# Four heads' 64-key remainders as one unit, and scales for two pairs of heads at once, in a fused attention and MoE kernel

## The chip, the cores and the metric

The kernel runs on one core of a Trainium2 chip. The metric is the device time of one execution in microseconds; the profile shows one such execution, engine by engine. The engines are TensorE (PE for its matmuls, PEld for its weight loads), VectorE (DVE), ScalarE (ACT), GpSimd (POOL) and SyncE (SP), whose queue issues nearly all DMAs. Each engine works through its own queue in order; between engines, semaphores hold an instruction back until what it reads has been written and the buffer that it writes is free.

## What is computed

Attention with a sigmoid in the place of the softmax, for 8 batches, 12 heads, 448 positions and 64 elements per head, and behind it a layer of two matrix products with an odd function between them:

```
scores = matmul(q, k.T) / sqrt(64) - log(448)
attn   = 1 / (1 + exp(-scores))
x      = matmul(attn, v)            # heads side by side: 3584 x 768
h      = x @ w_in                   # 768 x 2048
out    = (h - tanh(h)) @ w_out      # 2048 x 768
```

All arrays are float32.

## The kernel before

**Precision.** A product is made of float16 parts: each operand is scaled by a power of two and split into a high and a low half, and three products (high with high, high with low, low with high) are summed. The scale comes from the operand's sum of squares. In batch 0, and for the products with the attention weights of batch 1, float32 matmuls are used.

**Stages.** Batch 0's attention (`attention32`) and its first layer (`moe1_32`) run while the weights arrive and are converted. From then on the stages alternate: the first layer of a batch (`moe1`, 54.6 us) and its second layer (`moe2`). The attention of the *next* batch runs inside the second layer: a generator, `stream`, yields after each block of attention, and `second` calls it at fixed steps of the second layer. A step is six matmuls on the output tile `po`; a stage has 48 of them, three groups of 16, and then a remainder, `por`. The table `BLOCKS = (8, 12, 16, ..., 52)` sets the steps of the twelve blocks of a batch; tables of their own serve the second layers of batches 0 and 1. So the order of the work is written by hand, on TensorE, ScalarE, VectorE and GpSimd alike; only SyncE's queue is ordered by the build.

**A pair of heads.** Two heads of 64 elements fill the 128 partitions, and attention goes by pairs, numbered g. The 448 keys of a pair are cut into three chunks of 128 keys (c = 0, 1, 2) and a remainder of 64 (c = 3). For a chunk, `scores` issues for each of the three products one matmul per head: 64 rows of the array each, all 128 columns, into a PSUM tile `sc` of two banks. For the remainder each head has one corner of the array, 64 rows by 64 columns, so that the two heads use two corners of four, and fill one bank of `sc`. `weigh` (L386) takes the sigmoid on ScalarE, `split_a` makes the halves `ahl` (L393 on ScalarE, L394 on VectorE), and `av` multiplies them with V into the PSUM tile `acc`; there too the remainder uses two corners of four. `evac_x` moves `acc` to memory and squares it.

**Two blocks a pair.** In the first block of pair g stand the chunks 0 and 1, the product with V of all four parts of pair g-1, its `evac_x`, the float16 parts of Q of pair g+1 (`parts`, L346 and L349) and those of V. In the second stand `scales` of pair g+2, the chunk 2 and the remainder of pair g, the parts of K of pair g+2, and the sums of squares of pair g+3 (`norms`, L316: ScalarE, three instructions).

**Parts and scales.** `parts` writes both halves into a tile `w`, of which there is one buffer for K and Q alike (`tag="w", bufs=1`), and a DMA (L351) transposes it into `K` or `Q`. The high half of Q is always written by ScalarE (L346), that of K by VectorE (L348) from batch 2 on; the low half by VectorE (L349). `scales` (L324 to L337) adds a pair's sums over the partitions with a small matmul into the PSUM tile `pbn`, which ScalarE reads (L326), and makes the scales with five small operations on VectorE. The sums that it uses were taken a whole pair earlier.

**Between the groups of 16 steps**, ScalarE (L823) and VectorE (L824) empty the two `po` tiles; `po` has two buffers in all, and the next group needs both.

Of the kernel before, what the change touches and what calls it, by code (L numbers as in the profile page):

```python
# [19 lines left out]
P = 128  # L20
# [14 lines left out]
class Builder:  # L35
# [254 lines left out]
    def load_v(self, b, j, pool, tag, bufs):  # L290
        t = pool.tile([P, 2 * QT + 1, D], F32, name="vn", tag=tag, bufs=bufs)
        for h in range(2):
            src = self.v[b, 2 * j + h]
            self.nc.sync.dma_start(
                t[:, h * QT : (h + 1) * QT], src[: QT * P].rearrange("(c p) d -> p c d", c=QT)
            )
            self.nc.sync.dma_start(t[h * D : (h + 1) * D, 2 * QT], src[QT * P :])
        return t
# [8 lines left out]
    def norms(self, loaded):  # L307

        n = len(loaded)
        ss = self.sums.pop(0)  # L310
        self.sums.append(ss)
        for i, t in enumerate(loaded):
            flat = t.rearrange("p a b d -> p (a b d)" if i < 2 else "p a d -> p (a d)")
            rows, size = flat.shape
            junk = self.sm.tile([P, 8 * D], BF16, name="sqn", tag="sq", bufs=4)
            self.nc.scalar.activation(junk[:rows, :size], flat, AF.Square, accum_out=ss[:rows, i : i + 1])  # L316
        return ss[:, :n]

    def scales(self, ss):

        nc = self.nc
        n = ss.shape[1]
        pb = self.ps.tile([P, 512], F32, name="pbn", tag="tr", bufs=1)[:, :n]
        nc.tensor.matmul(pb, self.onesf, ss, start=True, stop=True)  # L324
        t = self.sm.tile([P, 3], F32, name="tn")
        nc.scalar.activation(t[:, :n], pb, AF.Relu, bias=self.tiny, scale=2.1)  # L326
        y = self.pow2(t[:, :n], n, "n")
# [4 lines left out]
        r = self.sm.tile([P, 2], F32, name="rn", bufs=5)  # L332
# [23 lines left out]
    def prep_v(self, vn, s):  # L356
        nc = self.nc
        flat = vn.rearrange("p c d -> p (c d)")
        v = self.att.tile([P, 2, 2 * QT + 1, D], F16, name="vhl", tag="vhl", bufs=3)
# [5 lines left out]
    def scores(self, c, K, Q):  # L365

        nc = self.nc
        ps = self.ps.tile([P, 2, 512], F32, name="sc", tag="sc", bufs=2)
        prods = ((0, 0), (0, 1), (1, 0)) if K.dtype == F16 else ((0, 0),)
        for n, (w, x) in enumerate(prods):  # L370
            for h in range(2):
                r = slice(h * D, (h + 1) * D)
                o = ps[:, h, : self.S] if c < QT else ps[r, 0, : self.S]
                nc.tensor.matmul(  # L374
                    o,
# [66 lines left out]
    def stream(self):  # L442
# [10 lines left out]
        def load(g):  # L453
            if g < G:
                qk[g] = self.load_qk(*at(g))
                if splits(g):
                    v[g] = self.load_v(*at(g), self.nat, "vn", 2)
# [528 lines left out]
```

## Time and profile before

| | |
|---|---|
| median of 3 runs | 1251.36 us (1249.97 to 1251.57) |
| the profiled execution | 1252.35 us, of which the span from the first to the last instruction is 1250.0 us |
| mean granted clock of TensorE | 0.993 of full speed |
| PE busy | 97% of the span |
| DVE, ACT busy | 74%, 73% |
| first layer of a batch | 54.6 us |
| second layer with the attention of the next batch | 87.8 us |

The page gives the busy time of each engine, and the chain of work that ended last, followed back from the last instruction. A row of a group names the line, the engine, the operation, what it writes and reads, and how often; then the busy time, the mean of one, and the idle time just before them with what ended it. A row of the timeline gives start and length in us and, in brackets, the idle time of the engine before it and what ended that. A matmul's length in such a row is that of its way through the array; the next one starts long before it ends, so rates are read from starts.

### The profile page before, as it was taken

How to read it: one execution, taken by the hardware profiler on the slowest of the kernel's cores; microseconds unless marked ns; L12 is line 12 of the kernel's file. 1: busy time of each engine (PE TensorE's matmuls, PEld its weight loads, DVE VectorE, ACT ScalarE, POOL GpSimd, SP SyncE). 2: the span in 40 equal slices, each digit the busy share in tenths (PEclk: the TensorE clock that was granted, in tenths of full speed). 3: DMA queues.
4: the chain of work that ended last, by engine and by line, in shares of the span. 5: the costliest groups of instructions: out<-in, count | busy, mean ns of one | idle time of the engine just before them, and what ended most of it. 6: DMA issues, size and time to landing. Idle time of an engine off the chain costs nothing.

```text
span 1250.0 us, 20037 instructions
## 1 busy us (share of the span) xinstructions
PE 1209.4 (97%) x7675; PEld 627.3 (50%) x7675; DVE 920.4 (74%) x1476; ACT 910.7 (73%) x1325; POOL 37.8 (3%) x38
## 2 busy tenths in 40 slices
PE   9899878999999999999999999999999999999998
PEld 3234433455545555555555555555555555555555
DVE  4889987878965698667976689557975779636930
ACT  5767786968888688886887688786888767854820
POOL 0100000000000000100001000000000000000000
PEclk9999989999999999999999999999999999999999
DMA  8973358220044300542034400552024400300000
GB/s 206 281 205 90 82 123 217 59 64 1 12 109 99 85 1 16 109 100 44 1 71 102 93 2 4 100 109 57 1 58 99 90 22 1 72 21 20 1 14 32
DMA packets 226448, 89.79 MB, mean 72 GB/s; under 512 B 214704, under 2 KB 216496, under 8 KB 226352
## 3 DMA queue, kind: packets, MB, share of 16 engines
q1 hardware_dynamic: 225424, 88.29, 30.2%
q8 instruction: 60, 0.98, 0.3%
q10 hardware_dynamic: 928, 0.23, 0.1%
q14 instruction: 36, 0.29, 0.1%
HBM read 58.20 MB, written 11.01 MB: 55 GB/s over the span
## 4 chain that ended last, share of the span: by engine, by line
PE 79%; ACT 7%; DVE 7%; DMA 3%; issue 2%; SPq 1%; DVEq 0%; ACTq 0%
PE ph L679 31%; PE po L794 26%; PE sc L374 7%; PE acc L405 7%; PE por L832 5%; PE ph L709 2%; ACT a L386 2%; DMA raw<-moe_w_in 1%; ACT wo L215 1%; DMA qn<-q 1%; DVE g L664 1%; DVE m L753 1%; DVE m L767 1%; DVE wo L218 1%; DVE m L764 1%
## 5 line engine op out<-in xcount | busy, mean ns | idle before, releaser
L794 PE MATMUL po<-wo,g 128*128 128x384 f16 x2304 | 394.1, 327 | 4.8 <-DVE o L824 2.6
L679 PE MATMUL ph<-xhl,wi 128*128 128x448 f16 x2016 | 382.6, 352 | 0.0
L794 PEld LDWEIGHTS <-g 128*128 128x128 f16 x2304 | 220.2, 98 | 180.9 <-issue 41.5
L679 PEld LDWEIGHTS <-wi 128*128 128x128 f16 x2016 | 196.7, 98 | 185.0 <-issue 1.8
L394 DVE SCALAR_TENSOR_TENSOR ahl<-a,ahl 128x896 f16<-128x896 f32 (+1 forms) x144 | 138.8, 1004 | 71.2 <-ACT ahl L393 71.2
L386 ACT ACTIVATE a<-sc,nls,rn 128x896 f32<-128x896 f32 (+1 forms) x168 | 163.5, 997 | 36.3 <-PE sc L374 34.4
L749 ACT ACTIVATE u<-ph,ih 128x896 f32<-128x896 f32 x64 | 64.3, 1005 | 94.6 <-PE ph L679 91.0
L374 PE MATMUL sc<-Q,K 64*128 64x448 f16 x1008 | 116.7, 356 | 8.8 <-ACT a L386 6.9
L393 ACT ACTIVATE ahl<-a 128x896 f16<-128x896 f32 (+1 forms) x144 | 114.7, 846 | 0.4 <-DVE n_y L98 0.4
L753 DVE SCALAR_TENSOR_TENSOR m<-ph,ihk,u 128x896 f32<-128x896 f32 x64 | 73.6, 1151 | 42.7 <-ACT th L751 42.4
L349 DVE SCALAR_TENSOR_TENSOR w<-qn,sn,w 112x512 f16<-112x512 f32 x42 | 31.5, 750 | 87.0 <-ACT w L346 87.0
L405 PE MATMUL acc<-ahl,vhl 128*64 128x448 f16 (+1 forms) x864 | 93.0, 356 | 0.4 <-DVE ahl L394 0.4
L663 ACT ACTIVATE g<-m,Sg 128x896 f16<-128x896 f32 x64 | 66.6, 1041 | 34.0 <-DVE m L767 28.7
L767 DVE COPY_PREDICATED m<-u,th 128x896 f32<-128x896 uint32 x64 | 77.4, 1209 | 6.9 <-DVE m L764 0.5
L664 DVE SCALAR_TENSOR_TENSOR g<-m,Sg,g 128x896 f16<-128x896 f32 x64 | 73.6, 1149 | 8.4 <-ACT g L663 8.3
L764 DVE SCALAR_TENSOR_TENSOR m<-q,m 128x896 f32<-128x896 f32 x64 | 69.9, 1093 | 9.9 <-ACT q L763 2.2
L709 PE MATMUL ph<-x,wi 128*128 128x448 f32 x192 | 75.1, 540 | 0.3 <-DVE x L417 0.3
L374 PEld LDWEIGHTS <-K 64*128 64x128 f16 x1008 | 41.3, 97 | 66.5 <-issue 39.3
L754 DVE SCALAR_TENSOR_TENSOR th<-ph,ih,th 128x896 f32<-128x896 f32 x64 | 73.4, 1147 | 0.0
L766 ACT ACTIVATE u<-u,b 128x896 f32<-128x896 f32 x64 | 66.7, 1043 | 5.9 <-DVE m L753 4.0
L760 DVE SCALAR_TENSOR_TENSOR m<-q,m 128x896 f32<-128x896 f32 x64 | 69.7, 1089 | 0.0
L405 PEld LDWEIGHTS <-vhl 128*64 128x64 f16 (+1 forms) x864 | 42.7, 108 | 48.7 <-issue 26.7
(131 smaller groups left out, 1228.3 us busy)
## 6 DMA issues: line engine op xcount, KB each, us to landing
raw<-moe_w_in SPq DMA_DIRECT2D x24, 512.0 KB, 5.9
rawo<-moe_w_out SPq DMA_DIRECT2D x32, 384.0 KB, 4.1
kn<-k SPq DMA_DIRECT2D x96, 112.0 KB, 2.8
qn<-q SPq DMA_DIRECT2D x94, 112.0 KB, 2.9
vn<-v SPq DMA_DIRECT2D x96, 96.0 KB, 2.5
out<-o SPq DMA_DIRECT2D x21, 384.0 KB, 2.4
vn<-v SPq DMA_DIRECT2D x96, 16.0 KB, 2.2
out<-orem SPq DMA_DIRECT2D x16, 96.0 KB, 2.2
```

The source lines that it names most:

```text
L374: nc.tensor.matmul(o, K[r, w, c * P : min((c + 1) * P, self.S)], Q[r, x, :], start=(n == 0), stop=(n == len(prods) - 1),)
L386: self.nc.scalar.activation(a, ps[:, :n, : self.S], AF.Sigmoid, bias=self.nls, scale=scale)
L393: nc.scalar.activation(A[:, 0], a, AF.Copy, scale=A_SCALE)
L394: nc.vector.scalar_tensor_tensor(A[:, 1], a, A_SCALE, A[:, 0], op0=ALU.mult, op1=ALU.subtract)
L405: self.nc.tensor.matmul(acc[o, : self.S], v[k, w, j], A[k, x, i], start=(c == 0 and n == 0), stop=(c == QT and n == len(prods) - 1),)
L664: nc.vector.scalar_tensor_tensor(g[:, 1], m, Sg, g[:, 0], op0=ALU.mult, op1=ALU.subtract)
L679: nc.tensor.matmul(ph[:, e, :S], self.wi[:, c * self.NB + k, part, e * P : (e + 1) * P], xhl[c][:, x, :], start=(i == 0), stop=(i == 3 * s ...
L709: nc.tensor.matmul(ph[:, e, :S], self.where("in", c)[:, f * P : (f + 1) * P], xs[c], start=(c == 0), stop=(c == self.NC - 1),)
L753: V.scalar_tensor_tensor(m, ps, ihk, u, op0=ALU.mult, op1=ALU.mult)
L764: V.scalar_tensor_tensor(m, q2, C2, m, op0=ALU.add, op1=ALU.mult)
L767: V.copy_predicated(m, u.bitcast(U32), th)
L794: nc.tensor.matmul(po[i][:, :H], gs[f // 2][:, x, f % 2, tk * P : (tk + 1) * P], self.wo[:, i * self.NF + f, w], start=(f == 0 and n == 0) ...
```

## The change

Attention goes by two pairs of heads, g (even) and h = g+1.

- The remainders of the two pairs are one unit: the four heads' 64 keys take the four corners of the array, head by rows and pair by columns, and fill both banks of one `sc` tile. Sigmoid and halves work on a full tile. In the product with V the four corners add into two `acc` tiles, of g and h, open at the same time: that of an even pair in the PSUM buffer `av`, that of an odd pair in `tr`.
- The remainder of h is computed with g's, in g's second block; so K and Q of h have to be there by then.
- One call of `scales` serves two pairs; the larger of the two sums sets the scale. Its `pbn` lies in the buffer `av` (for batch 1 in `sc`).
- V's remainder rows of both pairs are loaded with the even pair's tile.
- The blocks are still two a pair, at the same steps. Per two pairs there are now four, called B1 to B4 here:

```
B1  chunks 0, 1 of g;  product with V of h-2 (three chunks);  evac of h-2;  parts of V of h;  sums of V of g+2
B2  chunk 2 of g and the four-corner unit;                                   sums of K, Q, V of g+3
B3  scales of g+2 and g+3;  chunks 0, 1 of h;  product with V of g and of the unit;  evac of g;  parts of K, then Q, of g+2
B4  chunk 2 of h;  parts of K, then Q, of g+3;  parts of V of g+2;  sums of K, Q of g+4
```

The core of the diff:

```diff
@@ scores
-        for n, (w, x) in enumerate(prods):
-            for h in range(2):
-                r = slice(h * D, (h + 1) * D)
-                o = ps[:, h, : self.S] if c < QT else ps[r, 0, : self.S]
...
+        m = P // len(K)
+        for n, (w, x) in enumerate(prods):
+            for i in range(len(K)):
+                for h in range(2):
+                    r = slice(h * D, (h + 1) * D)
+                    self.nc.tensor.matmul(
+                        ps[i * m : (i + 1) * m, h, : self.S],
+                        K[i][r, w, c * P : c * P + m],
+                        Q[i][r, x, :],
...
@@ scales
+        nc.vector.tensor_tensor(u[:, :n], t[:, :n, 0], t[:, :n, 1], op=ALU.max)
...
@@ stream: the blocks
+        for g in range(0, G, 2):
+            h = g + 1
+            early = not splits(g)
+            aa = units(g, (0, 1))
+            do_av()
...
+            prep_v(h)
+            keep(g, (0, 1), aa)
+            load(g + 3)
+            load_v(g + 3)
+            norm_v(g + 2)
+            yield 2750, True
+            aa = units(g, (2, QT))
+            if early:
+                do_av()
+            keep(g, (2, QT), aa)
+            norms(g + 3)
+            norm_v(g + 3)
+            yield 2750, True
+            scales(g + 2, "sc" if early else "av")
+            aa = units(h, (0, 1), lambda: parts_k(g + 2))
+            do_av()
+            keep(h, (0, 1), aa)
+            parts_q(g + 2)
+            load(g + 4)
+            yield 2750, True
+            aa = units(h, (2,), lambda: parts_k(g + 3))
+            if early:
+                do_av()
+            keep(h, (2,), aa)
+            parts_q(g + 3)
+            prep_v(g + 2)
+            load_v(g + 4)
+            norms(g + 4)
+            yield 2750, True
```

(`keep` calls `split_a`, `units` calls `scores` and `weigh`, and runs the parts of K between the sigmoids.)

Three places of the order are needed further on. The first is ScalarE's queue around the copies into `w`, in the second layer of batch 4. Before, with the rows of one pair (`sqn` is a sum of squares, `a32` a sigmoid, `x32` and `x2` the evac, `ahl` a half, `tn` the reading of `pbn`):

```order
L316 ACTIVATE sqn_8150,ss1_114<-kn_7536 112x512
L316 ACTIVATE sqn_8152,ss1_114<-qn_7539 112x512
L316 ACTIVATE sqn_8154,ss1_114<-vn_7542 128x448
L386 ACTIVATE a32_8194<-sc_8180,nls_96,rn_7372 128x896
L346 ACTIVATE w_8196<-qn_7307,sn_8116 112x512
L386 ACTIVATE a32_8201<-sc_8187,nls_96,rn_7372 128x896
L421 ACTIVATE x32_8228<-acc_8203,rn_7181 128x448
L430 ACTIVATE x2_8230<-x32_8228 128x448
L393 ACTIVATE ahl_8236<-a32_8194 128x896
L393 ACTIVATE ahl_8239<-a32_8201 128x896
L823 ACTIVATE o_8277<-po0_8046,iK_8044 128x384
L326 ACTIVATE tn_8283<-pbn_8281,tiny_104 128x3
```

and now, the end of B3, all of B4 and the start of the next B1:

```order
L399 ACTIVATE ahl_8151<-a32_8105 128x896
L399 ACTIVATE ahl_8154<-a32_8112 128x896
L353 ACTIVATE w_8157<-qn_7303,sn_8086 112x512
L393 ACTIVATE a32_8199<-sc_8192,nls_96,rn_7227 128x896
L399 ACTIVATE ahl_8206<-a32_8199 128x896
L353 ACTIVATE w_8209<-qn_7978,sn_8086 112x512
L316 ACTIVATE sqn_8222,ss1_114<-kn_8162 112x512
L316 ACTIVATE sqn_8224,ss1_114<-qn_8165 112x512
L393 ACTIVATE a32_8264<-sc_8250,nls_96,rn_8088 128x896
L393 ACTIVATE a32_8266<-sc_8257,nls_96,rn_8088 128x896
L429 ACTIVATE x32_8286<-acc_8133,rn_7227 128x448
L438 ACTIVATE x2_8288<-x32_8286 128x448
```

Before, one copy into `w` stood in every second block; now two stand in B3 and B4 with one sigmoid and one half between them, and none in B1 and B2. The second place is VectorE's queue at the same point, before:

```order
L348 TENSOR_SCALAR w<-kn,sn 112x512
L349 SCALAR_TENSOR_TENSOR w<-kn,sn,w 112x512
L394 SCALAR_TENSOR_TENSOR ahl<-a_8135,ahl 128x896
L394 SCALAR_TENSOR_TENSOR ahl<-a_8142,ahl 128x448
L349 SCALAR_TENSOR_TENSOR w<-qn,sn,w 112x512
L361 TENSOR_SCALAR vhl<-vn,sn 128x448
L362 SCALAR_TENSOR_TENSOR vhl<-vn,sn,vhl 128x448
```

and now:

```order
L355 TENSOR_SCALAR w<-kn,sn 112x512
L356 SCALAR_TENSOR_TENSOR w<-kn,sn,w 112x512
L400 SCALAR_TENSOR_TENSOR ahl<-a_8105,ahl 128x896
L400 SCALAR_TENSOR_TENSOR ahl<-a_8112,ahl 128x896
L356 SCALAR_TENSOR_TENSOR w<-qn,sn,w 112x512
L355 TENSOR_SCALAR w<-kn,sn 112x512
L356 SCALAR_TENSOR_TENSOR w<-kn,sn,w 112x512
L400 SCALAR_TENSOR_TENSOR ahl<-a_8199,ahl 128x896
L356 SCALAR_TENSOR_TENSOR w<-qn,sn,w 112x512
L368 TENSOR_SCALAR vhl<-vn,sn 128x512
```

K of the second pair (its L355) now follows Q of the first directly in the queue, into the same `w`. The third is ScalarE's queue ahead of the reading of `pbn`, now (B2 and the first row of B3; before, as the rows above show, the sums of squares ahead of a `tn` belonged to a later pair than the `tn`):

```order
L903 ACTIVATE o_8010<-po0_7805,iK_7803 128x384
L393 ACTIVATE a32_8034<-sc_8014,nls_96,rn_7227 128x896
L393 ACTIVATE a32_8036<-sc_8021,nls_96,rn_7227 128x896
L399 ACTIVATE ahl_8038<-a32_8034 128x896
L399 ACTIVATE ahl_8041<-a32_8036 128x896
L316 ACTIVATE sqn_8044,ss0_112<-kn_7975 112x512
L316 ACTIVATE sqn_8046,ss0_112<-qn_7978 112x512
L316 ACTIVATE sqn_8048,ss0_112<-vn_7981 128x384
L329 ACTIVATE tn_8078<-pbn_8076,tiny_104 128x6
```

The last sums into `ss0` now stand directly ahead of the `pbn` that adds them up.

273 lines of the change are left out of this document (148 added, 125 removed).

## The prediction

> **What bounds the kernel now.** First the page: which engine is full, and what the chain of waits that ended last is made of.
>
> ```profile
> PE 1209.4 (97%) x7675; PEld 627.3 (50%) x7675; DVE 920.4 (74%) x1476; ACT 910.7 (73%) x1325; POOL 37.8 (3%) x38
> PE 79%; ACT 7%; DVE 7%; DMA 3%; issue 2%; SPq 1%; DVEq 0%; ACTq 0%
> ```
>
> TensorE is the bound over the whole. The change lies in the second layers, so I look there: busy time by stretches (length, then PE, PEld, DVE, ACT and POOL busy with counts, the granted clock, DMA), for the second layer of batch 3 and for two pairs of heads in it.
>
> ```profile
> 624.24:712.01 87.77, 87.77 (x688) 47.69 (x686) 60.42 (x114) 71.57 (x118) 4.54 (x4) 1.00 0.38 85
> 647.00:673.48 26.48, 26.48 (x198) 14.05 (x197) 15.79 (x35) 21.63 (x38) 2.27 (x2) 1.00 0.47 105
> ```
>
> TensorE never pauses there. But ScalarE works 21.63 of 26.48 us: only 4.85 us of slack for two pairs. Next the chain in order of time, for one pair (start, length):
>
> ```profile
> 802.66 1.36 PE sc L374 x12
> 804.01 4.01 PE po L794 x24
> 808.02 1.24 PE sc L374 x12
> 809.26 2.51 PE acc L405 x24
> 811.77 4.01 PE po L794 x24
> ```
>
> It is TensorE's own work, end to end: 13.13 us and some 0.1 us for `pbn`.
>
> **What TensorE saves.** The timeline of the same pair shows what a remainder costs.
>
> ```profile
> 667.12 0.33 PEld L405 LDWEIGHTS <-vhl 64*64 64x64 f16 x6 [0.36 <-issue]
> 667.81 3.69 PEld L794 LDWEIGHTS <-g 128*128 128x128 f16 x24 [0.36 <-issue]
> 671.73 0.28 PE L324 MATMUL pbn<-ss,onesf 128*128 128x3 f32 x2
> 671.94 1.43 PE L374 MATMUL sc<-Q,K 64*128 64x448 f16 x12
> 672.61 0.33 PEld L374 LDWEIGHTS <-K 64*64 64x64 f16 x6 [0.37 <-issue]
> 673.29 0.76 PEld L794 LDWEIGHTS <-g 128*128 128x128 f16 x6 [0.36 <-issue]
> ```
>
> From the first weight load of a remainder to the next work: 0.68 us for scores (672.61 to 673.29), 0.69 for the product with V; `pbn` takes 0.2 (671.73 to 671.94). Two corners run side by side already. No row shows four: if they do too, two pairs lose one remainder of each kind and one `pbn`, 0.68 + 0.69 + 0.2 = 1.5 us, and TensorE needs 25.0 us where it needed 26.5. If the corners went two by two, it would save 0.2. I take the first, since two heads on two disjoint corners cost no more than one pass. That is 6% of the cycle, if the other engines keep up.
>
> **What the new order asks of ScalarE.** Its rows, with those of VectorE and of SyncE's queue that it depends on:
>
> ```profile
> 661.09 1.41 ACT L393 ACTIVATE ahl<-a 128x896 f16<-128x896 f32 x2
> 662.39 0.62 ACT L316 ACTIVATE sqn<-kn 112x512 bf16<-112x512 f32 x1
> 664.09 0.19 ACT L316 ACTIVATION_READ_ACCUMULATOR sqn<-vn 128x1 f32 x1
> 665.30 2.58 PE L405 MATMUL acc<-ahl,vhl 128*64 128x448 f16 x24
> 665.85 0.71 ACT L346 ACTIVATE w<-qn,sn 112x512 f16<-112x512 f32 x1
> 666.59 0.75 DVE L349 SCALAR_TENSOR_TENSOR w<-qn,sn,w 112x512 f16<-112x512 f32 x1 [2.90 <-ACT w L346]
> 667.37 1.22 SPq L351 DMA_TRANSPOSE Q<-w  x1
> 667.74 0.68 DVE L362 SCALAR_TENSOR_TENSOR vhl<-vn,sn,vhl 128x448 f16<-128x448 f32 x1
> 667.92 0.63 ACT L421 ACTIVATE x<-acc,rn 128x448 f32<-128x448 f32 x1 [0.38 <-PE acc L405]
> 669.13 1.77 ACT L393 ACTIVATE ahl<-a 128x896 f16<-128x896 f32 x2
> 670.10 2.29 DVE L394 SCALAR_TENSOR_TENSOR ahl<-a,ahl 128x896 f16<-128x896 f32 x2 [1.67 <-ACT ahl L393]
> 672.72 1.71 ACT L386 ACTIVATE a<-sc,nls,rn 128x896 f32<-128x896 f32 x2 [0.23 <-PE sc L374]
> 673.44 0.49 DVE L348 TENSOR_SCALAR w<-kn,sn 112x512 f16<-112x512 f32 x1
> 673.96 0.75 DVE L349 SCALAR_TENSOR_TENSOR w<-kn,sn,w 112x512 f16<-112x512 f32 x1
> ```
>
> The last fact is how long a transpose holds `w`: the DMA issues (count, median us from issue to landing):
>
> ```profile
> K<-w SPq DMA_TRANSPOSE x42, 3.0
> Q<-w SPq DMA_TRANSPOSE x42, 3.0
> ```
>
> ScalarE loses a little work. Two sigmoids of half a tile become one full one: 2 x 1.71 for full and half twice, against about 3.1 for three full, 0.3 saved; the halves likewise 2 x 1.41 against 2.6, 0.2; one reading of `pbn`, 0.25. 21.6 becomes 20.8 us.
>
> But `w` has one buffer, and four fillings of it, K and Q of g+2 and of g+3, now follow each other within B3 and B4. From ScalarE's copy for Q of g+2 to its copy for Q of g+3 stand, one behind the other: copy 0.71, low half 0.75, transpose 3.0 until `w` is free, K 1.27 (673.44 to 674.71), transpose 3.0, and starts of 0.03 to 0.06 between. That is 8.9 us; VectorE's two `ahl` rows ahead of the low half add about 0.7 more. All that ScalarE has in between is one sigmoid and one half, 1.9 us, and it has to wait for B4's scores first. Behind the waiting copy stand the sums of g+4 and all of the next B1. So ScalarE stands still for some 6 us per two pairs at that place alone, and has a slack of 4 to 5.
>
> The delay then meets three things on which TensorE waits: the emptying of `po` (L823, in front of B2), the sums in B2 (the `pbn` of B3 needs those of K, Q and V of g+3, which now end directly before it), and the reading of `pbn` itself, because `acc` of g opens in the buffer where `pbn` lies. The trace has a small case of this:
>
> ```profile
> 774.45 1.43 PE L374 MATMUL sc<-Q,K 64*128 64x448 f16 x12
> 776.62 1.70 ACT L386 ACTIVATE a<-sc,nls,rn 128x896 f32<-128x896 f32 x2
> 784.25 0.72 ACT L346 ACTIVATE w<-qn,sn 112x512 f16<-112x512 f32 x1 [1.86 <-DMA K<-w]
> 789.28 0.32 PE L794 MATMUL po<-wo,g 128*128 128x384 f16 x1 [0.17 <-ACT o L823]
> 790.88 1.30 PE L794 MATMUL po<-wo,g 128*128 128x384 f16 x7 [1.28 <-DVE o L824]
> ```
>
> One wait of ScalarE for `w` of 1.86 us came out, at the next `po`, as 1.45 us of TensorE.
>
> **The cycle of two pairs, laid end to end from these rows.** Zero is the start of `pbn` in B3, in us; within a dense queue a sigmoid counts 1.0, a half 0.84, an evac 1.2 (667.92 to 669.13), three sums 1.9 (662.39 to 664.28).
> ScalarE: `pbn` read 0.6; sigmoids 1.0 to 3.1; evac at the end of the product with V (2.6 after its start), 4.1 to 5.3; halves to 7.1; Q of g+2 to 7.7; sigmoid and half of B4 8.8 to 10.7.
> `w`: K issued 2.8, landed 5.8; Q's low half behind VectorE's two `ahl`, to 9.2, landed 12.25; K of g+3 to 13.55, landed 16.65.
> ScalarE: idle from 10.7 to 16.65; Q of g+3 to 17.3; sums of g+4 to 18.5; B1's sigmoids, evac and halves to 23.4; the sum of V (loaded only after VectorE's parts of V, about 23.9) to 24.5; `po` to 25.0; B2's sigmoids to 27.0, halves to 28.6, sums to 30.5. Then the next `pbn`.
> TensorE meanwhile: B4 at 8.0, B1 at 12.7, B2 at 19.7; the four-corner unit waits there for Q of g+3 (landed 21.25), `po` for its emptying until 25.4, `pbn` until 30.5.
> So the cycle becomes **30.5 us** where it was 26.5; ScalarE's 20.8 us of work and about 9.7 us of waits set it. From below it is bounded by work plus the one wait for `w`: 20.8 + 6.0 = 26.8.
>
> **The sum.** The twelve blocks of a second layer are now B4, B1 to B4, B1 to B4, B1 to B3. Its first block starts 7.8 us in (8 steps); there ScalarE comes 2.2 us late from the first layer (774.45 to 776.62), `w` is free, and only one filling lies before Q of g+3. By the same steps K of g+3 is written by 4.7 us behind that block's start (VectorE, too, has a rest of the first layer to do) and landed at 7.7; from there to the `pbn` it is 13.9 us, as from 16.65 to 30.5 above: 21.6. Then two cycles, and 8.0 us from the last `pbn` to the end (0.2 + 1.24 + 2.51 + 4.0). 7.8 + 21.6 + 61.0 + 8.0 = 98.4 us against 87.8: +10.6, in each of batches 2 to 5: **+43**.
> Batch 1 has blocks from step 4 on, three steps apart at first; laid out in the same way, B3 at step 7 waits about 3 us for the sums, the first `w` wait costs the rest, and the stage ends 13.5 us later: **+13.5**. In batch 6 the last two pairs prepare nothing: **+2.5**. In batch 0's second layer ScalarE and VectorE convert weights; their work covers part of a wait for `w`, and half a wait each in two places, less what the blocks save, is **+4** (between -2 and +12). The attention of batch 0 runs while weights arrive: **-1** (0 to -3).
>
> The clock adds to it. In batch 1's second layer TensorE paused for 0.98 and 1.28 us around a single matmul; then the granted clock was one half (0.50 in the second row's columns, which are length, PE busy, clock, DMA share and rate), and 23 matmuls of `po` took 5.58 us, where 24 take 4.01 in the chain above: 1.6 to 1.8 us lost.
>
> ```profile
> 359.00 0.32 PE L794 MATMUL po<-wo,g 128*128 128x384 f16 x1 [0.98 <-ACT o L823]
> 360.60 5.58 PE L794 MATMUL po<-wo,g 128*128 128x384 f16 x23 [1.28 <-DVE o L824]
> ```
>
> ```profile
> 362.00:364.00 2.00, 2.00 (x8) 0.50 0.41 125
> ```
>
> The new pause before `po` is about 3.4 us (22.0 to 25.4), some 16 times. 1.8 us of slower matmuls fall partly into the 1.1 us that TensorE would wait for `pbn` anyway: 0.7 left, and I count it for half of them, **+5** (0 to +25). The Trainium skill (TensorE: Matmul & The Clock Gate, Part 1) has the clock halved after an idle window of about 3.4 us; by that rule pauses of 0.98 and 1.28 us would not have tripped it, and the new ones only now and then, so that this term would be near 0. The trace went the other way there, and I keep the row.
>
> 1252.35 + 43 + 13.5 + 2.5 + 4 - 1 + 5 = 1319 us for a profiled execution; those lie 1.0 above the median, so about **1318 us**, slower by 5%.
>
> **The rivals.**
> *Slower, but little.* If the waits that I put beside the one for `w` (evac for the product, V's load, `pbn`) overlapped with it after all, the cycle is 26.8 us, 0.3 above before; two of these, and the smaller first part of a stage (about +2), make +2 to +4 a stage: 1252 + 4 x 3 + 6 + 4 = 1274, with a spread of 1258 to 1285. For it: the ends are inferred, not shown. Against: three waits of the cycle are in one queue, in order.
> *Faster.* ScalarE's queue keeps up: the transposes hold `w` shorter, or TensorE's buffers bridge the wait. Then 1.5 us fall away 17 times, and up to 6 us of batches 0 and 1 more: 1252 - 26 - 6 = 1220. For it: TensorE is the bound at 97%, and the waits for `w` are few now. Against: the median of 3.0 us twice, in order, against 1.9 us of cover.
> *The corners do not run four at a time.* Then TensorE's cycle is 26.3 instead of 25.0, and its pauses shrink; ScalarE's 30.5 stays, so the total moves by less than 5 us. Without the waits it would mean no change.
> *Worse.* The clock stays down through `pbn`, scores and product with V, 4 us of which lie on ScalarE's loop: 2 us more a cycle, 1318 + 32 = 1350.
>
> **How the numbers follow.** The forecast (1290 to 1337) 0.62; slower but little 0.15; worse 0.11; faster 0.08; no change, with the corners two by two and no waits, 0.04. The range reaches from 1265, into the little-slower case, to 1340. Within 0.2% (2.5 us) counts as the same, about what a measurement here can tell: faster 0.08, same 0.04, slower 0.88.
>
> **What would show it.** Right: ScalarE's copy for Q (now L353) idle before it for `DMA K<-w`, some 6 us, about 17 times, 80 to 110 us in all; `pbn` (L327) and `po` (now L874) of TensorE waiting for ScalarE's sums and L903; two-pair cycles of about 30 us; TensorE's busy share down to 90% or so; first layers unchanged at 54.6. The four-corner unit is right if its six or twelve matmuls take no longer than 0.7 us. Wrong: cycles of 25 us without pauses, or `w` landing long before ScalarE gets to it; then the copy was not where I put it, or something else in that queue was already later.

## The result, and the profile after

The changed kernel takes 1350.63 us (median of 4 runs, 1343.7 to 1354.76), the kernel before 1250.66 us: the ratio is 1.0794, with a 95% interval of 1.0747 to 1.0842. The prediction was 1318 us, with a range up to 1340. The direction was right, and the loss was 100 us where 67 had been forecast. The profiled execution of the changed kernel is the fastest of its four, 1343.7 us with a span of 1341.4, so the trace holds 91.4 of these 100 us.

The page of the changed kernel, busy time by engine:

```profile
PE 1220.2 (91%) x7633; PEld 622.4 (46%) x7633; DVE 910.6 (68%) x1376; ACT 902.5 (67%) x1262; POOL 37.9 (3%) x38
```

TensorE executes 42 matmuls fewer and is busy 10.8 us longer; VectorE and ScalarE are busy some 9 us less. TensorE's share fell from 97% to 91%. What TensorE waits for, and what ScalarE waits for, is in the list of waits (waiting line, what ended the wait; us in all, times, the longest):

```profile
ACT w L353 <- DMA K<-w: 125.0, 27, 6.6
...
PE po L874 <- ACT o L903: 39.9, 14, 4.4
...
PE pbn L327 <- ACT sqn L316: 8.1, 7, 3.4
...
PE sc L382 <- DMA Q<-w: 5.6, 9, 1.4
```

The first row is the wait that the prediction named. The same wait in the kernel before:

```profile
ACT w L346 <- DMA K<-w: 12.6, 11, 2.1
```

Next two pairs of heads in the second layer of batch 4, from one `pbn` to the next. TensorE's rows of the timeline (start, length, instructions, and in brackets the idle time before them with what ended it):

```profile
858.10 0.30 PE L327 MATMUL pbn<-ss,onesf 128*128 128x6 f32 x2
...
873.84 4.07 PE L874 MATMUL po<-wo,g 128*128 128x384 f16 x24
877.85 0.74 PE L382 MATMUL sc<-Q,K 64*128 64x448 f16 x6
878.76 0.38 PE L382 MATMUL sc<-Q,K 64*64 64x448 f16 x2 [0.17 <-ACT a L393]
880.50 0.76 PE L382 MATMUL sc<-Q,K 64*64 64x448 f16 x10 [1.37 <-DMA Q<-w]
883.68 5.47 PE L874 MATMUL po<-wo,g 128*128 128x384 f16 x24 [2.42 <-ACT o L903]
889.06 0.39 PE L327 MATMUL pbn<-ss,onesf 128*128 128x6 f32 x2
```

and ScalarE's, in the same stretch:

```profile
868.01 0.95 ACT L399 ACTIVATE ahl<-a 128x896 f16<-128x896 f32 x1
874.79 0.72 ACT L353 ACTIVATE w<-qn,sn 112x512 f16<-112x512 f32 x1 [5.83 <-DMA K<-w]
...
883.07 0.56 ACT L903 ACTIVATE o<-po,iK 128x384 f32<-128x384 f32 x1
...
888.82 0.20 ACT L316 ACTIVATION_READ_ACCUMULATOR sqn<-vn 128x1 f32 x1
```

TensorE works end to end for 20.5 us. Then the four-corner unit waits for Q of g+3, `po` waits for its emptying, and the 24 matmuls of `po` behind these pauses take 5.47 us instead of 4.07. In ScalarE's queue the 5.83 us in front of the copy into `w` stand ahead of all that these pauses wait for; 0.86 us more went to a load of V, ahead of the emptying. The stretch is 30.96 us long.

The windows of the trace (length, then busy time of PE, PEld, DVE, ACT and POOL, granted clock, DMA share and rate) show this cycle, the two microseconds in which the clock was halved, and, last, batch 0's second layer:

```profile
858.10:889.06 30.96, 27.00 (x195) 13.83 (x194) 14.89 (x24) 21.17 (x34) 2.27 (x2) 0.94 0.39 88
884.00:886.00 2.00, 2.00 (x8) 0.96 (x7) 0.00 (x0) 2.00 (x3) 0.00 (x0) 0.50 0.50 197
...
149.10:290.10 141.00, 107.41 (x663) 48.15 (x661) 96.31 (x208) 94.87 (x177) 4.67 (x4) 0.88 0.40 101
```

The same view of the kernel before, for batch 0's second layer:

```profile
155.10:274.80 119.70, 104.41 (x669) 49.34 (x667) 98.51 (x219) 94.54 (x183) 4.55 (x4) 0.96 0.49 119
```

About the same work on VectorE and ScalarE, and 21.3 us more, of which TensorE is busy 3.0 us and idle 18.3 us. This is the stage for which the prediction had put +4.

Lengths of the second layers in us, read from the first and last starts of the first layers' `ph`, with those of the versions tried below (the first layers stay as they were, within 0.1):

| second layer of batch | before | changed | own `w` for Q | the same, `pbn` in `tr` | sums spread, V's last | the same, one `w` | GpSimd's loads |
|---|---|---|---|---|---|---|---|
| 0 | 119.7 | 141.0 | 132.9 | 131.0 | 137.3 | 141.5 | 129.7 |
| 1 | 98.1 | 118.4 | 105.1 | 105.6 | 93.5 | 111.3 | 94.0 |
| 2 | 88.1 | 101.9 | 92.7 | 92.9 | 84.0 | 99.1 | 84.1 |
| 3 | 88.0 | 100.4 | 91.6 | 91.0 | 83.8 | 99.2 | 84.0 |
| 4 | 89.6 | 100.4 | 91.6 | 91.9 | 83.8 | 99.3 | 83.8 |
| 5 | 88.1 | 101.4 | 90.1 | 90.1 | 83.8 | 104.0 | 83.8 |
| 6 | 81.8 | 87.2 | 80.5 | 80.7 | 77.7 | 87.2 | 77.4 |
| start to the last `ph` of batch 0 | 155.1 | 149.1 | 152.6 | 151.6 | 152.1 | 151.2 | 151.0 |
| median of the runs | 1250.7 | 1350.6 | 1281.7 | 1275.4 | 1239.6 | 1340.7 | 1232.7 |

### The profile page after: what moved, and what is told of

Read it like the earlier page. It is cut to its first block, busy times and chain, and to the rows that moved or that the text cites. A ratio compares the mean times of both kernels' runs of the same rounds, so it can differ in the third digit from the quotient of the medians.

```text
span 1341.4 us, 19713 instructions
## 1 busy us (share of the span) xinstructions
PE 1220.2 (91%) x7633; PEld 622.4 (46%) x7633; DVE 910.6 (68%) x1376; ACT 902.5 (67%) x1262; POOL 37.9 (3%) x38
## 4 chain that ended last, share of the span: by engine, by line
PE 55%; DMA 6%; ACT 6%; DVE 3%; issue 2%; SPq 1%; ACTq 0%; DVEq 0%
PE ph L759 24%; PE po L874 21%; PE sc L382 4%; PE acc L413 3%; PE por L912 3%; DMA K<-w 2%; DMA vn<-v 2%; ACT a L393 2%; ACT sqn L316 2%; DMA kn<-k 1%; DVE ahl L400 1%; ACT ahl L399 1%; DVE vhl L368 1%; ACT o L903 1%; SPq L297 1%
## 5 line engine op out<-in xcount | busy, mean ns | idle before, releaser
L874 PE MATMUL po<-wo,g 128*128 128x384 f16 x2304 | 419.8, 341 | 48.9 <-ACT o L903 39.9
L874 PEld LDWEIGHTS <-g 128*128 128x128 f16 x2304 | 229.0, 101 | 252.7 <-issue 123.0
L400 DVE SCALAR_TENSOR_TENSOR ahl<-a,ahl 128x896 f16<-128x896 f32 x126 | 137.6, 1125 | 129.9 <-ACT ahl L399 129.8
L393 ACT ACTIVATE a<-sc,nls,rn 128x896 f32<-128x896 f32 x147 | 154.5, 1089 | 30.9 <-PE sc L382 24.2
L382 PE MATMUL sc<-Q,K 64*128 64x448 f16 x1008 | 113.5, 376 | 22.6 <-ACT tn L329 9.6
L829 ACT ACTIVATE u<-ph,ih 128x896 f32<-128x896 f32 x64 | 64.4, 1006 | 84.1 <-PE ph L759 79.4
L353 ACT ACTIVATE w<-qn,sn 112x512 f16<-112x512 f32 x42 | 30.1, 716 | 125.0 <-DMA K<-w 125.0
L399 ACT ACTIVATE ahl<-a 128x896 f16<-128x896 f32 x126 | 113.2, 940 | 0.8 <-DVE m L847 0.2
L743 ACT ACTIVATE g<-m,Sg 128x896 f16<-128x896 f32 x64 | 66.7, 1042 | 36.1 <-DVE m L847 30.9
L413 PE MATMUL acc<-ahl,vhl 128*64 128x448 f16 (+1 forms) x864 | 81.8, 359 | 0.0
```

Of the source, the lines that this page charges most:

```text
L382: self.nc.tensor.matmul(ps[i * m : (i + 1) * m, h, : self.S], K[i][r, w, c * P : c * P + m], Q[i][r, x, :], start=(n == 0), stop=(n == len ...
L393: self.nc.scalar.activation(a[:, 0], ps[:, :, : self.S], AF.Sigmoid, bias=self.nls, scale=scale)
L399: nc.scalar.activation(A[:, 0], a[:, 0], AF.Copy, scale=A_SCALE)
L400: nc.vector.scalar_tensor_tensor(A[:, 1], a[:, 0], A_SCALE, A[:, 0], op0=ALU.mult, op1=ALU.subtract)
L413: self.nc.tensor.matmul(acc[i][h * D : (h + 1) * D, : self.S], v[k, w, 2 * QT + h if half else h * QT + c], A[k, x, h], start=(n == 0 and ...
L874: nc.tensor.matmul(po[i][:, :H], gs[f // 2][:, x, f % 2, tk * P : (tk + 1) * P], self.wo[:, i * self.NF + f, w], start=(f == 0 and n == 0) ...
```

## The experiments

**Theory A** was the prediction's: the one buffer of `w`, filled four times in a row, stops ScalarE, and what stands behind it in ScalarE's queue stops TensorE. The rivals: that ScalarE's queue, or the adjacency of sums and `pbn`, or a shared PSUM buffer, is the cause by itself; and that the four corners gain nothing.

### A buffer of its own for Q's w

```diff
@@ parts
-        w = self.qk.tile([CK, 2, 4 * P], F16, name="w", tag="w", bufs=1)
+        if name == "Q":
+            w = self.tp.tile([CK, 2, 4 * P], F16, name="w", tag="t")
+        else:
+            w = self.qk.tile([CK, 2, 4 * P], F16, name="w", tag="w", bufs=1)
```

> The changed kernel, with one thing altered: the halves of Q no longer go through the one buffer w but through a slot of the eight temporaries, so that ScalarE's copy for Q never waits for K's transpose, and K's never for Q's. Theory A (the wait for w sets the cycle): ScalarE's idle time before L353 falls from 125 us to under 10; the cycle of two pairs falls from about 31 to 25.5 to 26; second layers of batches 2 to 5 fall from about 101 to 86 to 88 us; the time falls by some 95 us, to 1235 to 1260. Rival B (the sums of squares that now end right ahead of pbn, and po's emptying behind them, hold TensorE whatever w does): the idle time moves to pbn and po, cycles stay at 29 or more, time 1310 or more. Rival C (the clock: TensorE is slow because it pauses, and a smaller pause still halves the clock): the waits go but po's 24 matmuls still take over 5 us behind each emptying; time about 1280.

Measured: 1281.69 us, ratio to before 1.0252 (1.0235 to 1.0269). This one buffer takes back 69 of the 100 us, and the wait of ScalarE's copy for `K<-w` is gone from the list. 31 us are left, above theory A's 1235 to 1260, so `w` is the largest cause and not the only one. The time is that of rival C, but not its sign: `po`'s matmuls take 395.7 us in all, against 394.1 before and 419.8 in the changed kernel. What is left has the sign of rival B: `pbn` waits 23.9 us for the sums, in 16 waits, and `po` 14.8 us for its emptying.

### Batch 1's pbn in another PSUM buffer, alone and with the above

```diff
@@ stream, B3
-            scales(g + 2, "sc" if early else "av")
+            scales(g + 2, "tr" if early else "av")
```

> The changed kernel, with pbn of batch 1's scales in the PSUM buffer tr and no longer in one of the two sc buffers. In batch 0's second layer TensorE's scores waited 9.6 us in three places for ScalarE to read pbn out of an sc buffer. Theory A (w sets that stage, 141 us long against 120 before): the stage gets shorter by 0 to 4 us, for ScalarE still stands 22 us at w there, and the time by no more than that. Rival D (pbn's place sets it): the stage falls by 8 to 10 us, time about 1340.

> Both: Q's halves through a temporary, and batch 1's pbn in tr. Theory A with D as a second, separate cause in batch 0's stage: that stage falls from 141 to 118 or less, the rest as with Q's halves alone, time 1230 to 1250, 5 to 10 below the kernel with Q's halves alone. If pbn's place was only a second wait behind that for w, no difference between the two (within 2 us).

Measured: 1346.96 us alone, 1.0768 (1.0743 to 1.0793), which cannot be told from the changed kernel. Batch 0's stage stays at 140.9 us: the wait for the reading of `pbn` has moved, from the scores to the unit's product (5.2 us in one wait), whose `acc` of the odd pair opens in `tr`. With Q's own buffer 1275.37 us, 1.0201 (1.0182 to 1.0220), 6.3 us below that buffer alone. That is a second, small cause. The stage is 131.0 us and not 118 or less, and the time not 1230 to 1250, so theory A lacks something there. What still holds TensorE and ScalarE in the latter version, from its waits:

```profile
ACT sqn L316 <- DMA qn<-q: 26.6, 12, 4.5
ACT sqn L316 <- DMA vn<-v: 26.0, 15, 3.1
PE pbn L327 <- ACT sqn L316: 24.2, 16, 3.4
...
PE po L877 <- ACT o L906: 14.9, 13, 2.6
```

`pbn` waits in each of its cycles for the sums that stand directly ahead of it, and the sums wait for their loads. The cycle is 26.9 to 28.6 us.

### The sums spread, and pbn away from acc

Pair g+3 is loaded a block earlier, its sums are spread over B4, B1 and the front of B2, V's parts of both pairs are made in B4 (from batch 2 on), and `pbn` lies in `tr` in all batches (in the second version in `av` from batch 2 on).

```diff
@@ stream, B1: from the version before
             aa = units(g, (0, 1))
+            if g:
+                norms(g + 2, (1,))
             do_av()
...
-            load(g + 3)
-            load_v(g + 3)
+            norms(g + 3, (0,))
             norm_v(g + 2)
@@ B2
             aa = units(g, (2, QT))
+            norms(g + 3, (1,))
+            norm_v(g + 3)
             keep(g, (2, QT), aa)
-            norms(g + 3)
-            norm_v(g + 3)
@@ B3
-            scales(g + 2, "tr" if early else "av")
+            scales(g + 2, "tr")
@@ B4
             parts_q(g + 3)
+            load(g + 5)
             prep_v(g + 2)
             load_v(g + 4)
+            prep_v(g + 3)
+            load_v(g + 5)
-            norms(g + 4)
+            norms(g + 4, (0,))
```

> Like the run before it (w of Q in a buffer of its own, 1275 us), and in addition the sums of squares no longer stand in one piece directly ahead of the matmul pbn: pair g+3 is loaded one block earlier, its sums of K and Q and those of V are spread over B4, B1 and the front of B2 (ahead of the halves), V's parts of both pairs are made in B4, and pbn lies in the PSUM buffer tr in all batches, so that acc of g does not open in the buffer that pbn's reading has to free. Theory A (the last 25 us are pbn waiting for the sums, 24 us in 16 waits, and po waiting for its emptying, 15 us, with the clock that these pauses cost): both waits go, the cycle of two pairs falls from 27.5 to 25.2-25.8 us, and the time to 1228-1245 us, below the 1250 of before. Rival B (ScalarE's dense queue itself, some 22 us of work a cycle, sets the cycle, and the waits only show it): 1262-1278 us, cycles above 27 us. Rival C (in part: the waits of po stay because B1 gets longer on ScalarE): 1245-1262 us.

> Like e5, but pbn of batches 2 on stays in the buffer av, where acc of g opens right behind it in B3. The reading of pbn now stands behind B2's halves on ScalarE, so acc should wait for it. Theory A (buffer sharing is a cost of its own): 0.5 to 1.5 us per cycle more than e5, 8 to 25 us in all. Rival: the same as e5 within 3 us, because ScalarE is through with the halves before TensorE is through with the scores.

Measured: 1273.87 us, 1.0185 (1.0162 to 1.0208), and with `pbn` in `av` 1274.91 us, 1.0191 (1.0168 to 1.0214). By the time, rival B: nothing gained. The waits of the first say that it was another thing:

```profile
PE po L884 <- ACT o L913: 20.8, 13, 3.1
...
PE por L922 <- ACT o L913: 6.2, 7, 1.7
...
PE pbn L327 <- ACT sqn L316: 3.5, 3, 1.5
...
ACT sqn L316 <- DMA vn<-v: 32.5, 16, 3.5
```

`pbn`'s wait did go, from 24.2 to 3.5 us. The sum of V of g+2, now in B1, waits for V's load, and the emptying of `po` stands right behind it. The wait had only moved to another place in the same queue. ScalarE's rows show it at one place, before `o`:

```profile
860.90 0.19 ACT L316 ACTIVATION_READ_ACCUMULATOR sqn<-kn 112x1 f32 x1
863.55 0.63 ACT L316 ACTIVATE sqn<-vn 128x512 bf16<-128x512 f32 x1 [2.47 <-DMA vn<-v]
864.09 0.19 ACT L316 ACTIVATION_READ_ACCUMULATOR sqn<-vn 128x1 f32 x1
864.18 0.56 ACT L913 ACTIVATE o<-po,iK 128x384 f32<-128x384 f32 x1
```

The place of `pbn` from batch 2 on makes no difference that can be measured.

### The order alone, with the single w

The rearranged order above, on the changed kernel's single `w`.

> The changed kernel with its single w, and with the spread sums and pbn in tr of e5 alone. Theory A (the chain of four fillings of one w delays ScalarE by some 6 us a cycle whatever the sums do; taking the second cause away alone gains little): 1315-1345 us, ScalarE's waits for K<-w still some 6 us, 17 to 27 times. Rival B (the wait for w costs only because the sums and the emptying of po stand behind it; with these out of the way it has cover): 1255-1295 us.

Measured: 1348.25 us, 1.0782 (1.0745 to 1.0819), which cannot be told from the changed kernel and lies just above theory A's 1315 to 1345. That the order alone gains little holds; even this little was overestimated.

### V's sums behind the sigmoids of B2; and the corners pair after pair

```diff
@@ stream, B1: from the version with the spread sums
             norms(g + 3, (0,))
-            norm_v(g + 2)
@@ B2
             norms(g + 3, (1,))
+            norm_v(g + 2)
             norm_v(g + 3)
```

> The last version (spread sums, pbn in tr, own buffer for Q's w) lost its wait at pbn, but its sum of V of g+2, which stood in B1 ahead of the emptying of po, waited 32.5 us in 16 waits for V's load, and po waited 20.8 us for the emptying. Here both sums of V stand in B2, behind the sigmoids. Theory A (these waits are what is left): po's waits go, cycles of 25.1-25.6 us, 1236-1250 us, so about the time of before or below. Rival B (ScalarE is simply too full, each wait taken away comes back elsewhere): cycles stay at 26-27 us, 1262-1276 us.

Measured: **1239.59 us**, ratio 0.9916 (0.9896 to 0.9937): 0.8% below the kernel before. One sum of 0.8 us, with its wait for V's load, moved past the emptying of `po`, is worth 34 us here. The windows of this version show the second layer of batch 3, in which TensorE is without a pause and at the full clock:

```profile
629.80:713.60 83.80, 83.77 (x683) 45.40 (x682) 58.17 (x98) 69.21 (x108) 4.53 (x4) 1.00 0.39 87
```

In these stages its cycles of two pairs take 25.0 to 25.2 us, and 25.6 the one with the token norms in it; TensorE's need had been predicted at 25.0. ScalarE has 69.21 us of work in 83.80, so it was never too full. Rival B falls.

For the second kernel the loops were exchanged, so that the unit issues all products of pair g and then all of pair h:

```diff
@@ scores, and av in the same way
-        for n, (w, x) in enumerate(prods):
-            for i in range(len(K)):
+        for i in range(len(K)):
+            for n, (w, x) in enumerate(prods):
```

> Like e8, but the four-corner unit issues all products of pair g first and then those of pair h, in the scores and in the product with V, so that only two corners at a time have work. Theory A (four corners run at the rate of one pass, as the prediction took it): six passes more per unit of two kinds, about 0.33 us each, 0.6-0.75 us a cycle where TensorE is the bound, 17 cycles and two early ones: 8-14 us slower than e8. Rival (four at a time was no gain, or ScalarE sets the cycle): within 3 us of e8. The rows of sc with 64x64 weights tell the first of these apart by themselves.

Measured: 1240.98 us, 0.9926 (0.9910 to 0.9942); the second layers of batches 2 to 5 are 83.8 to 83.9 us as before. The experiment did not do what it was meant to: the hardware still ran the four corners side by side. The first weight loads of a unit, in the version with the products interleaved (start, length):

```profile
813.37 0.33 PEld L385 LDWEIGHTS <-K 64*64 64x64 f16 x12 [0.37 <-issue]
```

and with the pairs one after the other:

```profile
814.60 0.35 PEld L385 LDWEIGHTS <-K 64*64 64x64 f16 x12 [0.37 <-issue]
```

Twelve loads in 0.35 us, where six took 0.33 before the change: the second pair does not wait for the first one's three products. So the rival that four corners gain nothing is refuted by the 0.33 us and the 25.0 us cycle, and not by this contrast.

### One w again, in the fastest version; and its fillings spread

```diff
@@ parts: as in the changed kernel
-        if name == "Q":
-            w = self.tp.tile([CK, 2, 4 * P], F16, name="w", tag="t")
-        else:
-            w = self.qk.tile([CK, 2, 4 * P], F16, name="w", tag="w", bufs=1)
+        w = self.qk.tile([CK, 2, 4 * P], F16, name="w", tag="w", bufs=1)
```

> The fastest version so far (spread sums, V's sums in B2, pbn in tr: 1239.6 us), but with the single w of the changed kernel for K and Q alike. Theory A (the four adjacent fillings of one w alone stop ScalarE for 5 to 6 us a cycle; its slack is now some 3 us): cycles of 27.5-30 us instead of 25.0-25.6, 1285-1330 us. Rival B (with the other waits gone ScalarE has enough slack to take the wait in): cycles under 26.5, 1240-1265 us. Rival C (nothing gained without w, as when the order alone was changed): 1335-1350 us.

Measured: 1340.68 us, 1.0718 (1.0691 to 1.0745), 101 us above the same kernel with two buffers. That is rival C's range; theory A's 1285 to 1330 was too low. ScalarE's wait, and what follows on TensorE:

```profile
859.43 0.95 ACT L399 ACTIVATE ahl<-a 128x896 f16<-128x896 f32 x1
866.23 0.72 ACT L353 ACTIVATE w<-qn,sn 112x512 f16<-112x512 f32 x1 [5.86 <-DMA K<-w]
```

```profile
870.76 0.76 PE L382 MATMUL sc<-Q,K 64*64 64x448 f16 x10 [0.45 <-DMA Q<-w]
874.15 0.32 PE L881 MATMUL po<-wo,g 128*128 128x384 f16 x1 [2.64 <-ACT o L910]
875.08 5.58 PE L881 MATMUL po<-wo,g 128*128 128x384 f16 x23 [0.61 <-DVE o L911]
880.49 0.28 PE L327 MATMUL pbn<-ss,onesf 128*128 128x6 f32 x2
```

No sum stands directly ahead of `pbn` here, and the cycle still takes 30.0 to 31.0 us in the stages of batches 2 to 4 (33.7 and 32.1 in batch 5's). The pauses of 0.45, 2.64 and 0.61 us and 1.6 us of slower matmuls are enough. In the cycle of the changed kernel shown above, the sums (888.82 + 0.20) and the slow `po` in front of `pbn` (889.06) end at the same time; that is why the order alone, with the single `w`, showed nothing.

Then the same with the fillings some 5 us apart, without any buffer more:

```diff
@@ stream, B1: from the version above (load_one loads K or Q alone)
             aa = units(g, (0, 1))
             if g:
+                parts_q(h)
+                load_one(g + 3, 1)
                 norms(g + 2, (1,))
@@ B4
-            aa = units(h, (2,), lambda: parts_k(g + 3))
+            aa = units(h, (2,))
             keep(h, (2,), aa)
-            parts_q(g + 3)
-            load(g + 5)
+            parts_k(g + 3)
+            load_one(g + 5, 0)
```

> As the last, with one w, but its fillings are spread: K of g+3 is written at the end of B4, behind the halves, and Q of g+3 only in the next B1, behind the sigmoids, so that K, Q, K, Q lie about 5 us apart instead of four in a row. No buffer is added. Theory A (what costs is that the fillings follow each other within the 4.5 us that one takes, not that there is one buffer): the wait for w on ScalarE falls below 2 us a cycle, the cycle to 25.2-26.5, the time to 1242-1265 us. Rival B (any single w is too slow, since 18 us of 25 are taken up by four fillings): 1280 us or more. Rival C (Q of g+3 lands too late for the four-corner unit in B2, and TensorE waits there): 1260-1280 us with a new wait of sc for Q<-w.

Measured: 1305.31 us, 1.0415 (1.0378 to 1.0451). Theory A falls: 35 us are taken back, not 76 or more. The time is in rival B's range, and the waits show rival C's mechanism beside ScalarE's old wait:

```profile
PE sc L382 <- DMA Q<-w: 45.0, 16, 4.5
...
ACT w L353 <- DMA K<-w: 40.2, 17, 5.3
```

Rival C has a mechanism that is there, and had its price too low; rival B is not excluded. So adjacency is only a part. The two orders tried with one `w` are both bad: filled early, it stops ScalarE; filled later, Q of the odd pair comes too late for the four-corner unit, which needs it a block earlier than the kernel before did. Whether a third order would do, no run shows.

### The loads of w_out in batch 0's second layer

```diff
@@ conv_load
-        self.nc.sync.dma_start(p["raw"], src[r * P : (r + 1) * P, i * n : (i + 1) * n])
+        queue = self.nc.sync if p["staged"] or not i else self.nc.gpsimd
+        queue.dma_start(p["raw"], src[r * P : (r + 1) * P, i * n : (i + 1) * n])
```

> The fastest version (1239.6 us), with the sixteen late loads of w_out (rawo) in batch 0's second layer issued by GpSimd's queue instead of SyncE's. That stage takes 137 us where it took 119.7 before. Theory A (the loads stand in SyncE's queue behind transposes and loads of V that wait for other engines, so the matmuls on the converted weights, wl, come late): the waits of wl for stb, 15 us there, fall below 6 us, the stage to 122-130 us, the time to 1225-1234 us. Rival B (the loads wait for their buffers, or the scales' reading tn behind the weight splits on ScalarE sets the stage): within 4 us of 1239.6. Rival C (GpSimd's own adds, which wait for ScalarE, hold the loads back): slower by up to 10 us.

Measured: **1232.69 us**, 0.9856 (0.9841 to 0.9871), 1.4% below the kernel before, and the stage 129.7 instead of 137.3 us. TensorE's waits in this stage, first with SyncE's queue and then with GpSimd's:

```profile
PE wl L178 <- DVE stb L152: 14.8, 4, 5.3
```

```profile
PE wl L179 <- DVE stb L153: 3.9, 4, 2.0
```

The same edit on the changed kernel, and on the kernel before:

> The changed kernel, with nothing else altered than that the sixteen late loads of w_out are issued by GpSimd's queue. Theory A (in batch 0's second layer these loads stand behind SyncE's waits for transposes and V): that stage falls from 141 us by 5 to 10, the time to 1338-1347. Rival (there the waits for w hide the loads): within 3 us of 1350.

> The same edit on the kernel before. Theory A (the delay of the loads comes from the change's bunched transposes and loads, and before it there was little of it): 1247-1252 us, gain under 3. Rival (the loads were as late before, and the edit is a general gain): 1241-1246 us; then the 7 us that it gained in the rearranged version are not a part of what the change cost.

Measured: 1353.87 us, 1.0826 (1.0805 to 1.0846), the stage 144.6 us; and 1252.11 us, 1.0011 (1.0001 to 1.0021). The edit helps neither; theory A of the first, 1338 to 1347, is refuted. The kernel before had nothing to gain there, and in the changed kernel the loads are not what the stage waits for. The stage had grown from 131.0 to 137.3 us with the rearranged order, so the 7 us are put down to that order; no run moves the loads with Q's own buffer and the old order.

Last, the fastest version with the changed kernel's order of sums and loads for batch 1's pairs:

> The fastest version (GpSimd's queue for the loads, 1232.7 us), but batch 1's pairs, whose attention is prepared in the stages of batch 0, keep the changed kernel's order of sums and loads (sums of V of g+2 in B1, all of g+3 at the end of B2, loads of K and Q in B1); the rearranged order is used from batch 2 on. Theory A (the rearrangement costs 6 us in batch 0's second layer, as 131.0 against 137.3 us said): that stage 123-127 us, 1226-1231 us. Rival (the 6 us came from the loads of w_out behind the rearranged loads in SyncE's queue, which are out of the way now): 1231-1237 us.

Measured: 1232.07 us, 0.9854 (0.9840 to 0.9869), the stage 129.5 us. That is the rival's range: with the loads out of the way the rearranged order costs nothing there.

## Why the prediction was wrong in size

**The mechanism, right.** The list of what would show it came out: 125 us of waits for `K<-w` in 27 (80 to 110 forecast, in about 17), `po` and `pbn` waiting for ScalarE, TensorE's share at 91%, first layers unchanged, the twelve weight loads of a unit within 0.33 us. So did the reckoning of the cycle. From the start of `pbn`, in us: the copy for Q of g+3 at 16.7 (forecast 16.65), the unit after its wait for Q at 22.4 (21.25), `po` at 25.6 (25.4), the next `pbn` at 31.0 (30.5). That a buffer, and not ScalarE's load, was the cause was shown in both directions: Q's own `w` takes back 69 us, and the single one put into the fastest version costs 101.

**Batch 0's second layer: the step that failed.** +21.3 us against +4 (and outside its own -2 to +12). With 21.3 in the place of 4 the same sum comes to 1335 us, inside the range, so this is the term that failed. The step said that the conversion of weights on ScalarE covers part of a wait for `w`, and counted two half waits. The timeline of ScalarE in the changed kernel has this:

```profile
170.88 0.72 ACT L353 ACTIVATE w<-qn,sn 112x512 f16<-112x512 f32 x1 [3.80 <-DMA K<-w]
...
172.44 1.10 ACT L215 ACTIVATE wo<-wo,swo_s 128x384 f16<-128x384 f32 x2
...
181.14 0.72 ACT L353 ACTIVATE w<-qn,sn 112x512 f16<-112x512 f32 x1 [6.61 <-DMA K<-w]
...
183.00 1.11 ACT L215 ACTIVATE wo<-wo,swo_s 128x384 f16<-128x384 f32 x2
...
219.13 0.72 ACT L353 ACTIVATE w<-qn,sn 112x512 f16<-112x512 f32 x1 [5.58 <-DMA K<-w]
...
245.63 0.90 ACT L215 ACTIVATE wi<-wi,swi_s 128x256 f16<-128x256 f32 x2
246.43 0.25 ACT L329 ACTIVATE tn<-pbn,tiny 128x6 f32<-128x6 f32 x1
```

Most conversions stand in the queue *behind* the waiting copies (at 183.00 for one) and are delayed with them. Ahead of the copy that waits 6.61 us stand only two (172.44, 1.10 us together). So they covered little: all waits of ScalarE for `K<-w` in this stage come to 22.3 us in 5, where two half waits had been counted. And at 246.43 the reading of `pbn` comes 8.4 us after the sums, behind seventeen splits of weights (237.91 to 246.43). TensorE needs it there, because `pbn` of batch 1 lies in a buffer of the scores; the prediction had weighed what `pbn`'s buffer holds up only where that is `acc`, from batch 2 on:

```profile
246.74 1.30 PE L382 MATMUL sc<-Q,K 64*128 64x448 f16 x6 [7.62 <-ACT tn L329]
```

Only a part of the 21.3 is settled. Q's own buffer took back 8.1; the place of `pbn` took back nothing alone, and another 1.9 with that buffer. With both, the stage still was 131.0, some 11 us above the old 119.7, and it stayed above that in every version (129.5 at best). Moving the loads of w_out alone took nothing off it. What is left in the last version is a wait of 5.3 us on the same reading of `pbn`, waits of 6.7 us in all for the converted weights and shorter ones of other kinds; no run takes them apart, so the cause of these 11 us stays open.

**Batch 1's, too small:** +20.3 against +13.5. It was laid out with one wait of 3 us for the sums and one for `w`; ScalarE waits there three times for `w`, 18.3 us in all. Q's buffer takes back 13.3 of it, the order 12.1 more.

**Batches 2 to 5, nearly right:** +13.8, +12.4, +10.8 and +13.3 against +10.6 each, 50.3 in all, against 43 (four times 10.6 is 42.4). The cycle was reckoned at 30.5 us and takes 30.9 to 32.3 in these stages. **Batch 6:** +5.4 against +2.5. **The start:** -6.0 against -1, the one term that was better than forecast; in the other versions the same stretch gains 2 to 4.5 us, so a part of this belongs to the one execution.

**The clock** was put at +5. `po` took 25.7 us more in all (419.8 against 394.1 us by groups), but in the cycle shown the slow matmuls end when the sums end, at 31.0 us, so they cost little there, as the prediction had it; with the sums out of the way the cycle is no shorter (30.0 to 31.0 us in most stages of the run with one `w`). Batch 0's stage, where the clock fell from 0.96 to 0.88, was not in that term.

**The median** lies 7 us above the profiled execution, where the step from one to the other had taken 1 us off. The changed kernel's executions spread over 11 us, those of the kernel before over 2. Why, no run shows.

**The rivals.** "Faster" (1220) did not come: the transposes hold `w` no shorter (3.0 us again). Its number is near what another kernel reaches: with a second buffer, and no load awaited ahead of `po`'s emptying, the cycle is 25.0 us and the time 1232. "Slower, but little" (26.8 us a cycle) was excluded by the version with one `w` and spread sums: the one wait is enough for 30 to 31 us. "The corners do not run four at a time" is refuted. "Worse" (1350) has the right total by luck: it had a cycle of 32.5 us and batch 0's stage at +4.

## What to carry to other kernels

Before an order of work is changed, list for each single-buffered tile between engines and a DMA how far apart its fillings lie, and compare that with the time from filling to landing; here that time was 4.5 us (copy 0.71, low half 0.75, transpose 3.0) with four fillings in a row, and a second buffer was worth 69 to 101 us where the saving that was sought was some 26. In an engine's queue, whatever waits for a DMA belongs behind what another engine is waiting for: one sum of 0.8 us that waited for its load, ahead of the emptying of `po`, cost 34 us. When a fix gains nothing, compare the waits and not the times, since the wait may have moved or another may end at the same moment; and cover is only what stands ahead of the waiting instruction in the queue.

## What the runs showed of the hardware

**A single pause of 1.68 us can halve the clock, and one of 1.79 us need not.** In the version with the spread sums, TensorE's rows for two waits on the emptying of `po`:

```profile
837.57 4.06 PE L884 MATMUL po<-wo,g 128*128 128x384 f16 x24 [0.70 <-ACT o L913]
...
864.79 5.77 PE L922 MATMUL por<-wo,g 128*64 128x384 f16 x48 [1.68 <-ACT o L913]
```

and the granted clock behind the second one:

```profile
866.00:868.00 2.00, 2.00 (x16) 1.51 (x14) 0.00 (x0) 2.00 (x6) 0.00 (x0) 0.50 0.50 197
```

After 0.70 us nothing is lost; after 1.68 us 48 matmuls take 5.77 us, where the version without pauses has:

```profile
847.64 4.09 PE L922 MATMUL por<-wo,g 128*64 128x384 f16 x48
```

So that pause costs itself and 1.7 us more. But the same execution has a longer one that costs nothing beyond itself; the granted clock behind it is 1.00:

```profile
982.80 4.06 PE L884 MATMUL po<-wo,g 128*128 128x384 f16 x24 [1.79 <-ACT o L913]
```

What tells the two cases apart, no run shows. The Trainium skill (TensorE: Matmul & The Clock Gate, Part 1) gives an idle window of about 3.4 us for this; this trace has the clock halved after about half of that, and the measurement decides.

**Corners run out of the program's order.** Twelve products issued as six of one pair and then six of the other have their weight loads within 0.35 us, like twelve issued in turn. A corner's work does not wait here for earlier work of another corner; so TensorE does not start such products strictly in the order of its queue, as the section on the chip had it for every engine.
